# Three value loads of batch 0 tied behind the third block's reciprocal, and that block's finish moved ahead of unit 1's turns

## The chip, the cores and the metric

The kernel runs on one core of one Trainium2 chip. The metric is the device time of one execution in microseconds, the median over several runs. One execution was also taken with the hardware profiler; its views are what the argument below reads.

## The reference

Sparse causal attention over chunks, then a gated feed-forward layer. Inputs are q, k, v of 4 batches, 8 heads, 768 positions, 64 dimensions, in float32, and three weight matrices.

```python
k_chunks = k.reshape(B, H, nc, 32, D)                     # nc = 24
ub = sum over d of max(q*k_min[chunk], q*k_max[chunk])    # an upper bound for each chunk
top_chunks = argsort(where(causal, ub, -1e9))[..., -6:]   # six chunks of each query
scores = where(chosen & causal, (q @ k.T) / 8, -1e9)
attn = softmax(scores);  x = attn @ v                     # -> x: 3072 tokens x 512
out = (sigmoid(x @ w_gate) * (x @ w_val)) @ w_out         # 512 -> 1536 -> 512
```

## The kernel before, in words

**Tiling.** The 3072 tokens are cut into 8 units of 384 tokens, three blocks of 128 each. Unit 0 holds the first block of batches 0, 1 and 2 (the blocks that need no choice of chunks, since they see at most four). Unit 1 holds blocks 1 to 3 of batch 0. Unit 2 holds blocks 4 and 5 of batch 0 and the first block of batch 3; the rest follow.

**A first block** (function `first`) goes through these steps, with the names used below, `b` for the batch and `e` for one of two halves of the heads:

- `kf0_b`, `kf1_b`, `qf0_b`, `qf1_b`, `vf_b`: loads (issued by SP)
- `kfT_b`, `qfT_b`: turns on TensorE; `kf16_b`, `qf16_b`: casts; `scf_b`: scores; `expf_b_e`: exp (ScalarE, L751)
- `cmf_b_e`: the mask product, which sets what lies after the diagonal to zero (GpSimd, L753); `vc_b`: cast of the values (GpSimd)
- `pvf_b_e`: weights times values (TensorE, L760); `rzf_b_e`: reciprocal of the sums (VectorE, L766); `xf_b_e`: normalization (VectorE, L768)
- `xpsf_b_e`: turn (TensorE, L775); `xTf_b_e`: its eviction from PSUM into `xT_u0` (L452 on ScalarE, L454 on VectorE)

**Unit 1** is made ready at the same time: `k0_u1` to `k3_u1` and `q0_u1` to `q3_u1` are loads, `kn_`/`qn_` copies, `kT_`/`qT_` turns on TensorE, `kx0_`/`kx1_` minima and maxima (VectorE), `kt_`, `qf_`, `qm_`, `hk.._` and `hq.._` copies and casts. Its values are `v_0_1`, `v_0_2`, `v_0_3`: one load of 256 KB each (`load_v`, L667, SP), and one cast each (`v16_0_1` to `v16_0_3`, L673, GpSimd). The products `pv_u1_h` (L990) read them; of unit 1's heads, number 3 is the first in the order, after its mask product `cm_u1_3`.

**Weights** come by GpSimd's own DMA queue, with a cast from float32 to float16 on the way, in the order `wgp` (a quarter of the first third of w_gate), `wg0` (the rest of it), `wv0`, `wv1`, `wg1`, `wv2`, `wg2`, `wo0`, `wo1`, `wo2`. Everything else is loaded by SP's queue. Both queues use the same 16 DMA engines.

**The order** of all work is written out by hand: the string `ORDER` lists every operation with its engine (P TensorE, A ScalarE, V VectorE, G GpSimd, S SyncE, which issues loads and stores), and each engine runs its own in that order. `SLOTS` names each buffer. `TIES` adds waits: `a<b` makes the first instruction of `a` wait for the end of `b`:

```python
for b in ties.get(op.name, ()):
    tc.add_manual_dep(traced[n], ends[b], ..., reason="tie")
```

On SP the order around the change is: the loads of unit 1 (the last of them `k3_u1`, `q0_u1`, `k1_u1`), then `v_0_3`, `v_0_2`, `v_0_1`, `qf1_3`, `k0_u2`, `q2_u2`, `k1_u2`, and the other loads of unit 2. `fl_..` are products of constants that keep TensorE awake at the start.

Of the kernel before, what the change touches and what calls it, by code (L numbers as in the profile page):

```python
# [98 lines left out]
kf1_2=S kf0_1=S kfT_0=P kxf1=V fl_17=P fl_10=P fl_7=P kx0_u1_2=V kf16_0=V qf0_0=S qfT_0=P qf16_0=V qf1_1=S kf1_1=S kfT_1=P  # L99
kf16_1=V fl_15=P fl_16=P scf_0=P expf_0_1=A fl_19=P qf0_1=S qfT_1=P hq0=V ap1=V fl_14=P fl_9=P fl_13=P fl_11=P fl_18=P fl_12=P  # L100
qf16_1=V scf_1=P v10=G vf_0=S v16_0_0=G qf0_2=S qf1_2=S kf0_2=S expf_0_0=A cmf_0_0=G pvf_0_0=P rzf_0_0=V xf_0_0=V kx1_u1_2=V
cmf_0_1=G wgp=G kfT_2=P pvf_0_1=P qfT_2=P qf16_2=V rzf_0_1=V xf_0_1=V kxf0=V expf_1_0=A cmf_1_0=G vf_1=S vc_1=G pvf_1_0=P
rzf_1_0=V xpsf_0_0=P expf_1_1=A cmf_1_1=G pvf_1_1=P hkf0=G hk1_u1_2=A kf16_2=A scf_2=P expf_2_1=A expf_2_0=A k0_u1=S kn_u1_0=V
kT_u1_0=P xf_1_0=V fl_20=P fl_21=P wg0=G q3_u1=S qn_u1_3=A q2_u1=S rzf_1_1=V xf_1_1=V xpsf_1_1=P hq1=V xTf_1_1=V kx0_u1_0=V
kx1_u1_0=V vf_2=S wv0=G cmf_2_0=G fl_23=P xpsf_0_1=P fl_24=P fl_22=P fl_27=P xpsf_1_0=P vc_2=G xTf_1_0=V pvf_2_0=P rzf_2_0=V
xf_2_0=V q1_u1=S k3_u1=S kn_u1_3=G kT_u1_3=P hkp111=A q0_u1=S fl_28=P kx1_u1_3=V cmf_2_1=G pvf_2_1=P xpsf_2_0=P rzf_2_1=V xf_2_1=V
qT_u1_3=P qf_u1_3=V k1_u1=S qn_u1_1=A qT_u1_1=P xTf_0_0=A xTf_0_1=A qn_u1_2=A qn_u1_0=A kn_u1_1=G kT_u1_1=P kx1_u1_1=V kx0_u1_1=V
kt_u1_0=A qm_u1_3=A fl_25=P xpsf_2_1=P fl_26=P qT_u1_2=P v_0_3=S v_0_2=S v_0_1=S qf1_3=S k0_u2=S q2_u2=S k1_u2=S qf_u1_1=V
qf_u1_2=V v11=G wv1=G wg1=G hq0_u1_3=G qT_u1_0=P kt_u1_3=A hk0_u1_3=G hq1_u1_3=G wv2=G xTf_2_1=A xTf_2_0=A qf_u1_0=A qm_u1_0=A
g_u0_0=P g_u0_2=P kx0_u1_3=V kcr_f=V kcr_u1=V hkp101=V hq1_u1_0=V hkf1=V kt_u1_1=V hk0_u1_1=G wg2=G qm_u1_2=A qm_u1_1=A ub_u1=P  # L110
ubn0_u1=V ubm0_u1=V hq0_u1_1=A hq0_u1_2=A g_u0_3=P g_u0_1=P mx0_u1=V ap0_u1=V apt0_u1=V hqm0_u1_0=V v_u0_1=P v_u0_0=P v_u0_2=P
hq0_u1_0=A tanh_u0_2=A tanh_u0_1=A hg_u0_1=V ubn1_u1=V v_u0_3=P tanh_u0_3=A hg_u0_3=V ubm1_u1=V hg_u0_2=V tanh_u0_0=A hg_u0_0=V
# [257 lines left out]
sw0_u5_1<sw1_u5_0 sw1_u5_1<hg_u5_8 sw3_u5_2<c22_g4_u6 sw2_u5_2<c3_g2_u6 sw0_u45_1<c22_g2_u6 sw1_u45_1<c11_u5 sw0_u45_2<u4_u5  # L370
sw1_u45_2<c12_u5 sw3_u45_1<c22_u5 sw3_u45_2<c21_u5 tt0_u7<c11_u45 tt3_u7<c22_g1_u6 held_u6_2<hg_u6_8 sw2_u6_0<c11_g3_u7
sw2_u6_2<c4_g3_u7 sw1_u6_0<c12_g3_u7 sw2_u6_1<hg_u6_7 sw1_u67_0<sw0_u7_0 sw3_u7_0<hg_u7_4 sw1_u7_1<hg_u7_11 sw3_u7_2<sw1_u67_2
sw3_u67_2<c11_u7 sw3_u67_1<u4_u7 sw2_u67_2<c12_u7
"""


# [1080 lines left out]
```

## Time and profile before

| | |
|---|---|
| Median of 3 runs | 281.0 us (280.96 to 281.25) |
| Profiled execution, its own time | 279.88 us |
| Span of that execution, first to last instruction | 278.2 us |
| TensorE busy | 269.2 us (97%) |
| VectorE, ScalarE, GpSimd busy | 231.2, 180.4, 163.1 us |
| DMA moved | 34.70 MB, mean 125 GB/s |

In the rows below, times are microseconds from the start of the span. A row of the timeline gives start, duration, engine, line, operation, output and input, and how many instructions were merged (x3); in brackets stands the idle time before it and what ended it. PE is TensorE's matmul, PEld its weight load, DVE VectorE, ACT ScalarE, POOL GpSimd, SPq the issue of a DMA by SyncE. A DMA's time "to landing" counts from its issue to its last byte.

### The profile page before, as it was taken

The page shows a single profiled execution, that of the slowest core. Times are in us where ns is not written, and L with a number is a line of the kernel's source. Part 1 is how long each engine was busy: PE and PEld are TensorE (multiplying, and loading weights), DVE is VectorE, ACT ScalarE, POOL GpSimd, SP SyncE. Part 2 cuts the span into 40 slices and gives each one's busy share as a digit, 9 for nine tenths or more (in the row PEclk, how much of TensorE's full clock was granted, in tenths as well). Part 3 has the DMA queues.
Part 4 walks back from the last instruction along what each step waited for, and adds up shares of the span by engine and source line. Part 5 has one row for each costly group of instructions (what it writes and reads, how often), then busy time and mean ns, then how long its engine had stood idle before and what let it go on. Part 6 is the DMA issues. An engine that isn't in the chain of part 4 may idle for free.

```text
span 278.2 us, 7566 instructions
## 1 busy us (share of the span) xinstructions
PE 269.2 (97%) x2806; PEld 189.3 (68%) x2806; DVE 231.2 (83%) x686; ACT 180.4 (65%) x386; POOL 163.1 (59%) x262
## 2 busy tenths in 40 slices
PE   5979999999999999999999999999999999999995
PEld 3755658667755666557687657776888688778684
DVE  4799747687999998796999987978889998888985
ACT  6388969569858944468689979988983422341430
POOL 5797744639372873534669966724766467163440
PEclk9999999999999999999999999999999999999999
DMA  6999999999999598696896230100320033000304
GB/s 157 258 281 204 207 217 208 220 179 202 187 217 189 142 183 188 145 161 125 164 157 114 68 85 17 40 0 3 73 77 2 1 83 127 2 1 2 151 2 152
DMA packets 131717, 34.70 MB, mean 125 GB/s; under 512 B 119776, under 2 KB 128736, under 8 KB 131680
## 3 DMA queue, kind: packets, MB, share of 16 engines
q1 hardware_dynamic: 126912, 29.50, 50.6%
q0 software_dynamic: 4768, 4.72, 10.1%
q8 instruction: 22, 0.36, 0.5%
q14 instruction: 15, 0.12, 0.1%
HBM read 30.67 MB, written 6.29 MB: 133 GB/s over the span
## 4 chain that ended last, share of the span: by engine, by line
PE 87%; DMA 6%; DVE 5%; SPq 1%; issue 0%; POOL 0%; DVEq 0%
PE v_u L1259 20%; PE g_u L1259 15%; PE sc_u L957 12%; PE o_u L1308 11%; PE p_u L1082 10%; PE pv_u L990 7%; DMA wg<-in_moe_w_gate_dram 5%; PE p_g_u L1191 5%; PE ube_u L896 3%; DMA kf<-in_k_dram 1%; DVE xf L768 1%; PE kfT L709 1%; PE qfT L709 1%; PE fl L591 1%; DVE kx_u L681 1%; DVE kcr L681 1%
## 5 line engine op out<-in xcount | busy, mean ns | idle before, releaser
L968 ACT ACTIVATE att_u<-sc_u 128x512 f16<-128x512 f32 (+3 forms) x184 | 86.9, 573 | 8.6 <-PE sc_u L957 7.3
L1259 PE MATMUL v_u<-xT_u,wv 128*128 128x384 f16 x384 | 72.4, 326 | 0.0
L1280 DVE SCALAR_TENSOR_TENSOR hg_u<-gate_u,v_u 128x384 f16<-128x384 f16 x96 | 51.2, 545 | 19.3 <-ACT gate_u L1271 9.7
L1271 ACT ACTIVATE gate_u<-g_u 128x384 f16<-128x384 f32 x72 | 35.1, 499 | 40.3 <-PE g_u L1259 35.1
L1259 PE MATMUL g_u<-xT_u,wg 128*128 128x384 f16 x288 | 56.0, 326 | 0.9 <-ACT xT_u L452 0.5
L1259 PEld LDWEIGHTS <-wv 128*128 128x128 f16 x384 | 36.2, 98 | 20.3 <-issue 0.2
L974 POOL TENSOR_SCALAR_AFFINE_SELECT att_u<-att_u 128x384 f16<-128x384 f16 (+1 forms) x56 | 28.0, 509 | 37.4 <-ACT att_u L968 16.4
L1259 PEld LDWEIGHTS <-wg 128*128 128x128 f16 x288 | 26.7, 98 | 18.3 <-DMA wg<-in_moe_w_gate_dram 1.8
L1308 PE MATMUL o_u<-wo,hg_u 128*128 128x512 f16 x144 | 34.3, 379 | 0.0
L990 PE MATMUL pv_u<-v,att_u 128*128 128x65 f16 x640 | 26.3, 193 | 0.0
L990 PEld LDWEIGHTS <-att_u 128*128 128x128 f16 x640 | 24.2, 98 | 2.9 <-issue 0.6
L1228 DVE TENSOR_TENSOR f_g_u<-p_g_u,f_g_u 128x192 f32<-128x192 f32 (+1 forms) x72 | 24.9, 383 | 1.0 <-PE p_g_u L1191 0.4
L957 PE MATMUL sc_u<-hqe,hke 128*128 128x128 f16 (+2 forms) x220 | 25.1, 243 | 0.0
L957 PE MATMUL sc_u<-hqo,hko 128*128 128x128 f16 (+2 forms) x220 | 24.1, 243 | 0.0
L1308 PEld LDWEIGHTS <-hg_u 128*128 128x128 f16 x144 | 13.7, 98 | 13.4
L957 PEld LDWEIGHTS <-hke 128*128 128x128 f16 x220 | 16.5, 98 | 4.9 <-issue 0.6
L957 PEld LDWEIGHTS <-hko 128*128 128x128 f16 x220 | 16.4, 98 | 4.4
L673 POOL CAST v<-v 128x512 f16<-128x512 f32 x23 | 14.4, 627 | 5.8 <-DVE qf_u L863 1.8
L1271 ACT ACTIVATE gate_u<-f_g_u 128x384 f16<-128x384 f32 x24 | 11.9, 519 | 5.6 <-DVE hg_u L1280 2.9
L1011 DVE TENSOR_TENSOR x_u<-pv_u,rz_u 128x384 f16<-128x384 f32 (+1 forms) x28 | 14.6, 524 | 0.9 <-DMA xT_u<-x_u 0.6
L919 DVE MAX8 mx_u<-ubn_u 128x8 f32<-128x8 f32 (+16 forms) x152 | 12.7, 158 | 0.3
L1099 DVE SCALAR_TENSOR_TENSOR sw<-p_u,sw 128x256 f32<-128x256 f32 (+1 forms) x20 | 10.6, 528 | 2.4 <-PE p_u L1082 2.0
(187 smaller groups left out, 504.9 us busy)
## 6 DMA issues: line engine op xcount, KB each, us to landing
v<-in_v_dram SPq DMA_DIRECT2D x23, 256.0 KB, 4.7
k<-in_k_dram SPq DMA_DIRECT2D x12, 384.0 KB, 5.4
q<-in_q_dram SPq DMA_DIRECT2D x12, 384.0 KB, 5.9
out_dram<-osb_u SPq DMA_DIRECT2D x12, 256.0 KB, 3.3
out_dram<-sw SPq DMA_DIRECT2D x8, 256.0 KB, 2.1
wv<-in_moe_w_val_dram POOLq DMA_DIRECT2D x3, 512.0 KB, 9.8
wo<-in_moe_w_out_dram POOLq DMA_DIRECT2D x3, 512.0 KB, 17.6
qf<-in_q_dram SPq DMA_DIRECT2D x8, 128.0 KB, 3.3
```

The source lines that it names most:

```text
L673: plan.add(f"v16_{b}_{ib}", {POOL: pool(H * D)}, lambda e: nc.gpsimd.tensor_copy(v16[b % 2][:, ib, :, 0:D], at(t)), reads=[t], writes=[("v ...
L957: nc.tensor.matmul(at(t)[:, o:o + 128 * m], hk[b % 2][e_][:, p, 128 * jb:128 * jb + 128], hq[u.side][e_][:, p, 128 * x:128 * (x + m)], sta ...
L968: plan.add(f"exp_{u.name}_{h}_{y}", {ACT: act(n)}, lambda e, t=t, att=att, b0=b0, n=n: nc.scalar.activation(at(att)[:, b0:b0 + n], at(t), ...
L974: nc.gpsimd.affine_select(out=dv, in_=dv, compare_op=ALU.is_ge, fill=0.0, base=0, pattern=[[0, u.m], [1, 128]], channel_multiplier=-1)
L990: nc.tensor.matmul(at(pv)[:, last, x, :], at(att)[:, c:c + 128], v16[b % 2][:, jb, h, :], start=(jb == 0), stop=(jb == ib))
L1011: plan.add(f"x_{u.name}_{p}", {DVE: dve(u.t)}, lambda e: nc.vector.tensor_tensor(at(x_).rearrange("p a (e d) -> p e a d", e=2), at(pv)[:, ...
L1082: nc.tensor.matmul(at(to)[:, side], a(j)[:, i], b(j)[:, i], start=j == i == 0, stop=j == 2 and i == 1)
L1228: plan.add(f"{p}_{name}", {POOL: pool2(192 * n), DVE: dve(192 * n)} if slow else {DVE: dve(192 * n)}, lambda e: both(e).tensor_tensor(dst( ...
L1259: nc.tensor.matmul(at(t), w16[:, c, 128 * fb:128 * fb + 128], at(u.xt)[:, c, :], start=(c == 0), stop=(c == 3))
L1271: plan.add(f"tanh_{u.name}_{fb}", {ACT: act(T, not seven[0])}, lambda e, gv=gv, gate=gate: nc.scalar.activation(at(gate), gv(), AF.Tanh, s ...
L1280: plan.add(f"hg_{u.name}_{fb}", {DVE: dve(T)}, lambda e, vv=vv, gate=gate, hg=hg, fb=fb: nc.vector.scalar_tensor_tensor(at(hg)[:, fb % 2], ...
L1308: nc.tensor.matmul(at(o), at(hgs[fc // 2])[:, fc % 2, 128 * tb:128 * tb + 128], wo16[:, fc, lo:hi], start=(fc == 0), stop=(fc == NFB - 1))
```

## The change

One tie is added, `v_0_3<rzf_2_0`: the load `v_0_3`, and with it all that SP issues behind it, waits for the first reciprocal of the third block (batch 2). In `ORDER` the third block's operations move ahead of some of unit 1's, and `wgp` moves behind one mask product. By engine, before and after:

```
G  before: cmf_0_1 wgp cmf_1_0 vc_1 ... cmf_2_0 vc_2 kn_u1_3 cmf_2_1 kn_u1_1
   after:  cmf_0_1 cmf_1_0 wgp vc_1 ... cmf_2_0 vc_2 cmf_2_1 kn_u1_3 kn_u1_1
P  before: pvf_2_0 kT_u1_3 fl_28 pvf_2_1 xpsf_2_0 qT_u1_3 qT_u1_1 kT_u1_1 fl_25 xpsf_2_1 fl_26
   after:  pvf_2_0 fl_28 pvf_2_1 kT_u1_3 xpsf_2_0 qT_u1_3 xpsf_2_1 qT_u1_1 kT_u1_1 fl_25 fl_26
V  before: rzf_2_0 xf_2_0 kx1_u1_3 rzf_2_1 xf_2_1 qf_u1_3
   after:  rzf_2_0 xf_2_0 rzf_2_1 xf_2_1 kx1_u1_3 qf_u1_3
A  before: qn_u1_0 kt_u1_0 qm_u1_3 kt_u1_3 xTf_2_1 xTf_2_0 qf_u1_0
   after:  qn_u1_0 xTf_2_0 xTf_2_1 kt_u1_0 qm_u1_3 kt_u1_3 qf_u1_0
S  the same order
```

The diff, cut to the lines in which operations move:

```diff
-cmf_0_1=G wgp=G kfT_2=P pvf_0_1=P qfT_2=P qf16_2=V rzf_0_1=V xf_0_1=V kxf0=V expf_1_0=A cmf_1_0=G vf_1=S vc_1=G pvf_1_0=P
+cmf_0_1=G kfT_2=P pvf_0_1=P qfT_2=P qf16_2=V rzf_0_1=V xf_0_1=V kxf0=V expf_1_0=A cmf_1_0=G wgp=G vf_1=S vc_1=G pvf_1_0=P
...
-xf_2_0=V q1_u1=S k3_u1=S kn_u1_3=G kT_u1_3=P hkp111=A q0_u1=S fl_28=P kx1_u1_3=V cmf_2_1=G pvf_2_1=P xpsf_2_0=P rzf_2_1=V xf_2_1=V
-qT_u1_3=P qf_u1_3=V k1_u1=S qn_u1_1=A qT_u1_1=P xTf_0_0=A xTf_0_1=A qn_u1_2=A qn_u1_0=A kn_u1_1=G kT_u1_1=P kx1_u1_1=V kx0_u1_1=V
-kt_u1_0=A qm_u1_3=A fl_25=P xpsf_2_1=P fl_26=P qT_u1_2=P v_0_3=S v_0_2=S v_0_1=S qf1_3=S k0_u2=S q2_u2=S k1_u2=S qf_u1_1=V
-qf_u1_2=V v11=G wv1=G wg1=G hq0_u1_3=G qT_u1_0=P kt_u1_3=A hk0_u1_3=G hq1_u1_3=G wv2=G xTf_2_1=A xTf_2_0=A qf_u1_0=A qm_u1_0=A
+xf_2_0=V q1_u1=S k3_u1=S hkp111=A q0_u1=S fl_28=P cmf_2_1=G kn_u1_3=G pvf_2_1=P kT_u1_3=P xpsf_2_0=P rzf_2_1=V xf_2_1=V kx1_u1_3=V
+qT_u1_3=P xpsf_2_1=P qf_u1_3=V k1_u1=S qn_u1_1=A qT_u1_1=P xTf_0_0=A xTf_0_1=A qn_u1_2=A qn_u1_0=A xTf_2_0=A xTf_2_1=A kn_u1_1=G
+kT_u1_1=P kx1_u1_1=V kx0_u1_1=V kt_u1_0=A qm_u1_3=A fl_25=P fl_26=P qT_u1_2=P v_0_3=S v_0_2=S v_0_1=S qf1_3=S k0_u2=S q2_u2=S
+k1_u2=S qf_u1_1=V qf_u1_2=V v11=G wv1=G wg1=G hq0_u1_3=G qT_u1_0=P kt_u1_3=A hk0_u1_3=G hq1_u1_3=G wv2=G qf_u1_0=A qm_u1_0=A
...
-sw3_u67_2<c11_u7 sw3_u67_1<u4_u7 sw2_u67_2<c12_u7
+sw3_u67_2<c11_u7 sw3_u67_1<u4_u7 sw2_u67_2<c12_u7 v_0_3<rzf_2_0
```

## The prediction

> **What bounds the kernel now.** I read the page's busy times, then busy time by stretch, then the chain that ended last, then the timeline around the change, and last the landings of single loads.
>
> ```profile
> span 278.2 us, 7566 instructions
> PE 269.2 (97%) x2806; PEld 189.3 (68%) x2806; DVE 231.2 (83%) x686; ACT 180.4 (65%) x386; POOL 163.1 (59%) x262
> ...
> 0.00:36.00 36.00, 30.49 (x253) 20.36 (x254) 26.44 (x84) 25.64 (x52) 27.46 (x50) 1.00 1.08 221
> 36.00:120.00 84.00, 83.75 (x877) 54.35 (x875) 70.02 (x196) 56.40 (x128) 45.67 (x78) 1.00 1.01 189
> 120.00:200.00 80.00, 80.00 (x991) 55.51 (x990) 68.39 (x232) 70.49 (x144) 50.55 (x76) 1.00 0.43 82
> 200.00:278.20 78.20, 74.91 (x691) 59.09 (x689) 66.40 (x177) 27.87 (x65) 39.43 (x59) 1.00 0.16 55
> ```
>
> A stretch's row gives its length, then PE, PEld, DVE, ACT and POOL busy, the clock, the DMA share and GB/s. TensorE is the bound: of its 9.0 us idle, 5.5 lie before 36 us, 3.3 at the end, and 0.25 between 36 and 200. So a delay of TensorE near 36 us is hardly made up later. The DMA engines are full (share 1.01 and more) for the first 120 us: that is where a change in the order of loads can bite.
>
> ```profile
> 26.18 14.22 DMA wg<-in_moe_w_gate_dram
> 40.45 1.48 PE g_u L1259 x8
> ...
> 22.82 1.43 PE L1259 MATMUL g_u<-xT_u,wg 128*128 128x384 f16 x6 [0.51 <-ACT xT_u L452]
> 23.27 0.76 PEld L1259 LDWEIGHTS <-wg 128*128 128x128 f16 x6 [1.12 <-DMA wg<-in_moe_w_gate_dram]
> 22.00:26.00 4.00, 3.37 (x45) 1.42 (x44) 3.68 (x11) 3.96 (x11) 2.31 (x5) 1.00 1.22 206
> ```
>
> The chain passes through a load of w_gate that lands at 40.4, and unit 0's first gate products at 22.82 wait for the evictions of its x and for `wg0`. These are the waits that the change could shorten. Their whole worth is small: TensorE idles 0.63 us between 22 and 26, and 0.25 at 40.
>
> **The change part by part.** First, when the tie opens.
>
> ```profile
> 12.82 0.79 POOL L610 DMA_DIRECT2D wg<-in_moe_w_gate_dram  x1
> 12.86 1.08 ACT L751 ACTIVATE attf<-scf 128x512 f16<-128x512 f32 x2 [1.27 <-PE scf L746]
> 13.63 0.66 POOL L753 TENSOR_SCALAR_AFFINE_SELECT attf<-attf 128x512 f16<-128x512 f16 x1
> 15.91 0.80 POOL L612 DMA_DIRECT2D wg<-in_moe_w_gate_dram  x1
> 18.08 0.62 POOL L456 CAST vh<-vf 128x512 f16<-128x512 f32 x1
> 19.19 0.17 DVE L766 RECIPROCAL rzf<-pvf 128x4 f32<-128x4 f32 x1
> 19.79 0.56 DVE L681 TENSOR_REDUCE kx_u<-kT_u 128x12 f32<-128x384 f32 x1
> 22.13 0.65 ACT L452 COPY xT_u<-xpsf 128x256 f16<-128x256 f16 x2
> ```
>
> GpSimd issues `wgp` in the time in which it would wait for ScalarE's first exp of block 1, which ends near 13.40 (12.86 and half of 1.08). With `cmf_1_0` ahead, GpSimd starts it at 13.45 and `wgp` at 14.03, 1.2 us later; `vc_1` and all behind it, the issues of `wg0` and `wv0` too, come 0.6 us later (14.21 to 14.83), for GpSimd has no gap there up to the third block's value cast (18.08 to 18.70). Bound: 0 to 0.8, the issue's own 0.79. So `rzf_2_0`, which before ended at 19.36, ends at 20.0, and `v_0_3` goes out at 20.0 instead of 14.53. Behind it on SP stand the two other value loads, `qf1_3` and every load of unit 2.
>
> The moves on TensorE, VectorE and ScalarE bring the second half of block 2 forward past `kx1_u1_3` (0.56), a turn or two, and put two evictions (0.65 together) ahead of `kt_u1_0`, where ScalarE will also wait for their turns. I cost them at nothing: the next paragraphs show a wait of TensorE near 36 us that ends at a time set by a load, and whatever is won or lost before it only changes its length. If that cover is gone, they are worth between -0.6 (the idle time at 22 to 26) and +1.1 us (0.65 and some 0.4 of waiting).
>
> Now the loads.
>
> ```profile
> 14.53 4.84 SPq L667 DMA_DIRECT2D v<-in_v_dram  x3
> ...
> L667 SPq DMA_DIRECT2D v<-in_v_dram x1: 413/413/413, 14.5 to 14.5; - x1
> DMA to landing us min/median/max: 5.8/5.8/5.8
> ...
> L667 SPq DMA_DIRECT2D v<-in_v_dram x1: 3542/3542/3542, 15.8 to 15.8; - x1
> DMA to landing us min/median/max: 14.3/14.3/14.3
> ...
> L636 SPq DMA_DIRECT2D qf<-in_q_dram x1: 803/803/803, 19.5 to 19.5; - x1
> DMA to landing us min/median/max: 13.9/13.9/13.9
> ...
> L613 POOL DMA_DIRECT2D wv<-in_moe_w_val_dram x1: 780/780/780, 16.7 to 16.7; - x1
> DMA to landing us min/median/max: 9.8/9.8/9.8
> ...
> L613 POOL DMA_DIRECT2D wv<-in_moe_w_val_dram x1: 763/763/763, 20.4 to 20.4; - x1
> DMA to landing us min/median/max: 9.5/9.5/9.5
> ...
> 14.00:18.00 4.00, 2.39 (x32) 1.65 (x31) 3.65 (x12) 2.83 (x6) 4.00 (x7) 1.00 1.14 298
> ```
>
> `v_0_3` lands 5.8 us after its issue, before the bulk of the weights has begun to move: `wv0` lands at 26.5, `wv1` at 29.9. `v_0_1`, issued at 15.8 and let go by SP at 19.37, lands only at 30.1, and `qf1_3`, 128 KB behind it in the same queue, at 33.4. So once the weights run, SP's queue gets 128 KB through in 3.25 us, about 40 GB/s, where the engines moved 298 GB/s between 14 and 18. In the changed kernel `v_0_3` goes out at 20.0 and stands where `v_0_1` stood: it lands near 30.1. The two behind it need 6.5 us each: 36.6 and 43.1 for `v_0_1`. That is the late bound. The early bound: without the first two value loads in the way (512 KB, 1.7 us at 298 GB/s) `wg0` and `wv0`, themselves issued 0.6 later, are through up to 1.1 us sooner, while `wv1` can't be issued sooner; so the weights' queue may pause ahead of `wv1` for 0 to 1.1 us. In a pause the values pass at 298 GB/s; 1.1 us of it takes 328 KB, saves 8.2 us at 40 GB/s and costs 1.1, so `v_0_1` lands at 36.0. I take half of that pause, 0.5 us: 149 KB, 3.7 less 0.5, so 39.9.
>
> Who waits for it:
>
> ```profile
> 31.44 0.61 POOL L673 CAST v<-v 128x512 f16<-128x512 f32 x1
> 33.48 0.61 POOL L673 CAST v<-v 128x512 f16<-128x512 f32 x1 [0.74 <-DVE hqo L454]
> 34.20 0.99 POOL L974 TENSOR_SCALAR_AFFINE_SELECT att_u<-att_u 128x384 f16<-128x384 f16 x2
> 36.19 0.44 PE L990 MATMUL pv_u<-v,att_u 128*128 128x65 f16 x9
> ...
> 11.64 0.80 PE fl L591 x6
> ...
> L591 PE MATMUL fl<-ones x30: 269/396/421, 1.1 to 21.4; 128*128 128x256 f16 x30
> ```
>
> GpSimd casts `v_0_2` at 31.44 and `v_0_1` at 33.48; both will wait, and behind them on GpSimd stand `cm_u1_3` and `cm_u1_2` (34.20), without which `pv_u1_3` can't start, and TensorE runs in order. From the landing to `pv_u1_3`: the cast 0.61, a step of 0.11, one mask product 0.50, a step of 0.16, so 1.4 us. With 39.9 it starts at 41.3 instead of 36.19: **5.1 us**, between 1.2 (36.0) and 8.3 (43.1).
>
> A wait of 5 us may also cost TensorE its clock. The constant products took about 400 ns each at the start and 269 later, and the six at 11.64 took 133 ns apiece back to back: TensorE does start slow here. A restart after a long wait isn't in this trace. Bounds: 0, and half of the time from 1.1 to 11.64, 5.3. I take 1.5, near the low end, since after the wait TensorE is packed, while in its first ten microseconds it was fed in pieces. The Trainium skill (TensorE: Matmul & The Clock Gate, Part 1) says that about 3.4 us of idle time halve the clock and about 3.4 us of work restore it; by that this term would be an estimated 1.7 and the sum 0.2 higher.
>
> Off go TensorE's waits after 36 us that come from the weights: 0.25. The sum: 5.1 + 1.5 - 0.3 = +6.3 on the profiled execution's 279.88 (its span and 1.7 us around it), so 286.2. The median of the runs stands 1.1 above that execution: 281.0 + 6.3 = **287.3 us**.
>
> **The rivals.** *Faster: the values land in time.* If `v_0_1` lands by 34.8 (36.19 less 1.4), TensorE waits for nothing, and what is left is the shorter start: the idle 0.63 and 0.25 us at most, so 280.1. For it speaks that the first value load needed only 5.8 us, and that GpSimd asks for the last two 11.4 and 13.5 us after the new issue; against it, `v_0_1`'s 14.3 and `qf1_3`'s 13.9 us. It decides at a pause of 1.3 us or more in the weights' queue. The Trainium skill (DMA: Bandwidth & Descriptors, Anatomy of one DMA) fits a DMA at about 2.0 us and its bytes over 436 GB/s; by that fit, an estimate, the three would be in by 24 us and this rival would hold. The trace disagrees: 14.3 us for one such load beside the weights.
>
> *Slower still: unit 2's loads pile up too.*
>
> ```profile
> 40.97 0.40 POOL L456 COPY qn_u<-kq_u 128x256 f32<-128x256 f32 x1
> ...
> L647 SPq DMA_DIRECT2D kq_u<-in_q_dram x1: 1597/1597/1597, 23.1 to 23.1; - x1
> DMA to landing us min/median/max: 14.0/14.0/14.0
> ```
>
> `q2_u2` landed at 37.1, 7.0 us behind `v_0_1`; its copy on GpSimd began 7.5 us after the cast of `v_0_1`. Both move together, with 0.5 us to spare; if the queue spreads by half again (3.5 us) the turns of unit 2 wait 3 us more, and with the late bound the time is 281.0 + 8.3 + 1.5 + 3.0 - 0.3 = 293.5.
>
> *Nothing:* the tie opens before SP reaches the load. It would have to open by 14.53, and the third block's scores aren't even exponentiated then; 281.0.
>
> **How the numbers follow.** The forecast case, a wait of TensorE for `v_0_1`, holds 77 in 100: same queue, same neighbours, and the late landing is in the trace twice. Faster 13, pile-up 8, nothing 2. A measurement of this kernel can tell about 0.2%, 0.6 us, from no change. Faster 0.13; same 0.03, the last case and the edge of the first; slower 0.84. Range: the forecast's early bound (281.0 + 1.2 - 0.3 with no loss of clock, 281.9) to its late one with a clock loss of twice my value (281.0 + 8.3 + 3.0 - 0.3 = 292.0), drawn in to 282.0 and 291.5. It leaves out the faster case and most of the pile-up.
>
> **What would show it.** Right: the value loads issue near 20 us and land near 30, 35 and 40, where the first landed at 20 and the last at 30; GpSimd's third value cast waits for a DMA of v; TensorE idles some 5 us ahead of the `pv_u` products, is slow for a few microseconds behind it, and all later stretches are shifted and otherwise alike. `wg0` lands 1 to 2 us sooner, `wv1` not. Wrong: the third cast still near 34 us, or loads of v that land 7 us after their issue beside the weights; then the queue isn't shared as I read it.

## The result and the profile after

The changed kernel takes 283.7 us in the median of 21 executions (282.05 to 291.5), the kernel before beside it 281.0 (21 executions, 280.16 to 282.68). The ratio is 1.0075 [1.0057, 1.0092]; like every ratio below it leaves out executions that lie over 1.5% above the fastest of their kernel, here the seven above 287 (the medians stand 1% apart). So it is slower, as forecast, but by 2.7 us and not by 6.3.

The 21 times are two groups: 14 lie between 282.05 and 285.21, 7 between 287.55 and 291.5. The forecast of 287.3 falls into the gap. The profiled execution took 291.28 us and belongs to the upper group, so what it shows is the mechanism in its long form; profiles of the lower group follow with the repeats. First the page of the changed kernel:

```profile
span 289.5 us, 7563 instructions
PE 271.4 (94%) x2806; PEld 190.7 (66%) x2806; DVE 231.2 (80%) x686; ACT 180.4 (62%) x386; POOL 162.9 (56%) x262
```

Then its busy time by stretch, with the columns of before (length, PE, PEld, DVE, ACT, POOL, clock, DMA share, GB/s):

```profile
0.00:36.00 36.00, 30.34 (x253) 20.48 (x254) 26.54 (x84) 25.52 (x52) 23.96 (x43) 0.95 1.06 211
36.00:120.00 84.00, 74.90 (x759) 49.41 (x758) 60.81 (x163) 51.80 (x120) 43.91 (x78) 0.94 0.90 167
120.00:200.00 80.00, 80.00 (x974) 53.21 (x972) 68.35 (x238) 65.25 (x133) 49.09 (x72) 1.00 0.52 104
```

TensorE is busy for 30.34 us before 36 (before: 30.49) and without a gap from 120 to 200. In the second stretch it idles 9.1 us where it idled 0.25. The chain that ended last (start, duration, what) names the load:

```profile
16.16 4.64 DMA wg<-in_moe_w_gate_dram
20.80 23.54 DMA v<-in_v_dram
44.46 0.61 POOL v L673
45.07 0.48 POOL att_u L974
45.59 0.62 PE pv_u L990 x8
```

In the timeline stand the issue of the three value loads, their three casts, and what TensorE does behind them:

```profile
19.62 7.98 SPq L667 DMA_DIRECT2D v<-in_v_dram  x3
...
31.26 0.61 POOL L673 CAST v<-v 128x512 f16<-128x512 f32 x1 [1.37 <-DMA v<-in_v_dram]
...
37.95 0.61 POOL L673 CAST v<-v 128x512 f16<-128x512 f32 x1 [4.83 <-DMA v<-in_v_dram]
...
44.46 0.61 POOL L673 CAST v<-v 128x512 f16<-128x512 f32 x1 [5.21 <-DMA v<-in_v_dram]
...
45.59 0.62 PE L990 MATMUL pv_u<-v,att_u 128*128 128x65 f16 x8 [9.10 <-POOL att_u L974]
...
50.92 0.33 PE L1025 MATMUL xps_u<-ident,x_u 128*128 128x128 f16 x3
```

The loads go out from 19.6 and their casts follow one another by 6.7 and 6.5 us, each behind a wait for a DMA of v. TensorE's 9.10 us at `pv_u1_3` are the whole loss of its second stretch; the row names the mask product, which had itself waited for the cast, and the cast for the load. From `pv_u1_3` to the turns `xps_u1_3` it takes 5.33 us where before took 3.02, from 36.19 to this row of the kernel before:

```profile
39.21 0.33 PE L1025 MATMUL xps_u<-ident,x_u 128*128 128x128 f16 x3
```

The stretches of the changed kernel show the clock (the number before the DMA share), 0.80 in the wait and 0.50 behind it:

```profile
38.00:42.00 4.00, 0.00 (x0) 0.00 (x0) 0.00 (x0) 0.00 (x0) 1.25 (x2) 0.80 1.22 200
...
46.00:50.00 4.00, 4.00 (x25) 2.25 (x23) 1.82 (x5) 0.98 (x2) 1.15 (x4) 0.50 1.01 230
```

So this execution lost 9.4 us up to `pv_u1_3` and 2.3 us to the clock, 11.7 together, and ended 11.4 later than the profiled execution of before.

### The profile page after: what moved, and what is told of

Same layout as the page of the kernel before. It is cut to its first block, busy times and chain, and to the rows that moved or that the text cites. A ratio compares the mean times of both kernels' runs of the same rounds, so it can differ in the third digit from the quotient of the medians.

```text
span 289.5 us, 7563 instructions
## 1 busy us (share of the span) xinstructions
PE 271.4 (94%) x2806; PEld 190.7 (66%) x2806; DVE 231.2 (80%) x686; ACT 180.4 (62%) x386; POOL 162.9 (56%) x262
## 4 chain that ended last, share of the span: by engine, by line
PE 84%; DMA 11%; POOL 1%; DVE 1%; issue 1%; SPq 0%; ACT 0%; DVEq 0%; POOLq 0%
PE v_u L1259 20%; PE g_u L1259 15%; PE sc_u L957 12%; PE o_u L1308 11%; PE p_u L1082 9%; DMA v<-in_v_dram 8%; PE pv_u L990 7%; PE p_g_u L1191 5%; PE ube_u L896 2%; DMA wg<-in_moe_w_gate_dram 2%; DMA kf<-in_k_dram 1%; PE kfT L709 1%; PE qfT L709 0%; DVE ox L1099 0%; PE xps_u L1025 0%
## 5 line engine op out<-in xcount | busy, mean ns | idle before, releaser
L1280 DVE SCALAR_TENSOR_TENSOR hg_u<-gate_u,v_u 128x384 f16<-128x384 f16 x96 | 51.1, 544 | 29.3 <-ACT gate_u L1271 20.0
L1259 PE MATMUL v_u<-xT_u,wv 128*128 128x384 f16 x384 | 73.3, 329 | 0.0
L1259 PE MATMUL g_u<-xT_u,wg 128*128 128x384 f16 x288 | 56.7, 329 | 0.1
L1259 PEld LDWEIGHTS <-wv 128*128 128x128 f16 x384 | 36.6, 99 | 21.0 <-issue 1.2
L974 POOL TENSOR_SCALAR_AFFINE_SELECT att_u<-att_u 128x384 f16<-128x384 f16 (+1 forms) x56 | 28.0, 509 | 37.7 <-ACT att_u L968 17.5
L990 PE MATMUL pv_u<-v,att_u 128*128 128x65 f16 x640 | 26.9, 195 | 9.1 <-POOL att_u L974 9.1
L673 POOL CAST v<-v 128x512 f16<-128x512 f32 x23 | 14.4, 627 | 17.2 <-DMA v<-in_v_dram 11.4
L863 DVE STREAM_TRANSPOSE qf_u<-q 128x384 f32<-128x384 f32 (+2 forms) x28 | 11.7, 436 | 1.3 <-DMA q<-in_q_dram 1.2
```

What stands on the lines that cost most here:

```text
L974: nc.gpsimd.affine_select(out=dv, in_=dv, compare_op=ALU.is_ge, fill=0.0, base=0, pattern=[[0, u.m], [1, 128]], channel_multiplier=-1)
L990: nc.tensor.matmul(at(pv)[:, last, x, :], at(att)[:, c:c + 128], v16[b % 2][:, jb, h, :], start=(jb == 0), stop=(jb == ib))
L1259: nc.tensor.matmul(at(t), w16[:, c, 128 * fb:128 * fb + 128], at(u.xt)[:, c, :], start=(c == 0), stop=(c == 3))
L1280: plan.add(f"hg_{u.name}_{fb}", {DVE: dve(T)}, lambda e, vv=vv, gate=gate, hg=hg, fb=fb: nc.vector.scalar_tensor_tensor(at(hg)[:, fb % 2], ...
```

## The experiments

**The changed kernel again, three times.** They show the lower group, and how the sizes scatter.

> The changed kernel as it is, to see an execution that is not among its longest. Theory A (the value loads share the DMA engines with the weights, and the last of them lands at a time that differs from run to run): times spread between 282 and 291.5 us as before; in the profile the length of the wait ahead of the first pv_u product and the landing of the third value load move together: an execution of 283 us has the load landing near 36 to 38 and a wait of 1 to 3 us, with the granted clock hardly lowered. Theory B (the new order makes the start slower and the loads matter only now and then): the wait ahead of pv_u is nearly nothing in an execution of 283 us, and TensorE is behind already at 30 us by 2 us.

> The changed kernel once more, beside the kernel with constants ahead of pv_u and on the same chip. Theory A (a race between the value loads and wv1 on each DMA engine): short executions of 282 to 284.5 and about a third of 287 to 292, whichever chip.

> The changed kernel on the same chip, for comparison: 282 to 284.5, and long executions of 287 to 292 in up to a third.

Measured: 283.66 (281.8 to 292.15, 12 executions, 3 of them above 287), ratio 1.0058 [1.0027, 1.0088]; 283.15 (282.46 to 284.43, 6, none above 287), 1.0080 [1.0055, 1.0104]; 283.89 (282.02 to 291.73, 6, 2 above 287), 1.0096 [1.0062, 1.0131]. Their profiled executions took 283.51, 283.68 and 282.02. Timeline of the first, the same steps:

```profile
18.91 5.59 SPq L667 DMA_DIRECT2D v<-in_v_dram  x3
...
37.57 0.61 POOL L673 CAST v<-v 128x512 f16<-128x512 f32 x1 [4.81 <-DMA v<-in_v_dram]
...
38.70 0.42 PE L990 MATMUL pv_u<-v,att_u 128*128 128x65 f16 x8 [2.79 <-POOL att_u L974]
...
43.27 0.33 PE L1025 MATMUL xps_u<-ident,x_u 128*128 128x128 f16 x3
```

Of the second:

```profile
39.11 0.42 PE L990 MATMUL pv_u<-v,att_u 128*128 128x65 f16 x8 [2.58 <-POOL att_u L974]
...
42.11 0.34 PE L1025 MATMUL xps_u<-ident,x_u 128*128 128x128 f16 x3
```

And of the third:

```profile
20.03 4.71 SPq L667 DMA_DIRECT2D v<-in_v_dram  x3
...
37.91 0.42 PE L990 MATMUL pv_u<-v,att_u 128*128 128x65 f16 x8 [1.06 <-POOL att_u L974]
```

Where the last value load lands near 37 instead of 44, TensorE waits 1.06 to 2.79 us and not 9.10. Behind a wait of 2.79 the clock fell for a while (4.57 us to `xps_u1_3`, 1.55 more than before), behind 2.58 it did not (3.00); the last section shows that the length of the wait alone does not decide this. The granted clock of the stretch from 38 to 42 says the same, in the first and in the second repeat:

```profile
38.00:42.00 4.00, 3.30 (x26) 2.01 (x27) 1.11 (x3) 0.79 (x2) 2.26 (x6) 0.64 1.21 213
```

```profile
38.00:42.00 4.00, 2.89 (x32) 1.89 (x32) 1.17 (x4) 0.98 (x2) 2.68 (x6) 1.00 1.21 211
```

**The tie without the moves, and the moves without the tie.** The first is the kernel before with the tie, the second the changed kernel without it:

```diff
 before, one tie more:    +v_0_3<rzf_2_0
 after, that tie removed: -v_0_3<rzf_2_0
```

> The kernel before with the tie alone, the order as before. Theory A: the same delay of the value loads, opened some 0.3 us sooner (the reciprocal at 19.4): slower by 1 to 10 us, median 283 to 285, with a spread like the changed kernel's. Theory B: within 0.5 us of the kernel before.

> The changed kernel without the tie: the third block's operations stay ahead. Theory A: within 0.6 us of the kernel before, and a spread as small as its (280.2 to 282.7), since the value loads go out at 14.5 again. Theory B: 282.5 to 284, the changed kernel's time.

Measured: the tie alone 289.07 (283.33 to 290.94, 12), ratio 1.0116 [1.0074, 1.0159]; 7 of its 12 executions lie above 287. The moves alone 281.43 (280.42 to 282.85, 12), 0.9990 [0.9963, 1.0017]. The timeline of the tie alone, in its profiled execution of 290.94:

```profile
45.79 0.62 PE L990 MATMUL pv_u<-v,att_u 128*128 128x65 f16 x8 [9.32 <-POOL att_u L974]
```

So the whole loss comes from the tie, and the moves cost and bring nothing by themselves, although without the tie no wait hides them. With the tie, the moves made the upper group rarer (7 of 12 without them, 3 of 12 with them on the same chip); with such counts that is a hint and no more. The timeline of the moves alone:

```profile
37.14 0.43 PE L990 MATMUL pv_u<-v,att_u 128*128 128x65 f16 x9
...
40.16 0.33 PE L1025 MATMUL xps_u<-ident,x_u 128*128 128x128 f16 x3
```

This execution took 280.76, near the 281.0 of before, and `pv_u1_3` starts at 37.14, 0.95 later than in the profiled execution of before, with no wait for a value load. That matters below.

**How many of the three loads are held.** The kernel before, with the tie at the second or at the third load alone:

```diff
+v_0_2<rzf_2_0        (two loads held)
+v_0_1<rzf_2_0        (one load held)
```

> The kernel before with the tie on v_0_2: the first value load goes out at 14.9, two are held until 19.4. Theory A: 6.5 us less on the slowest DMA engine than with three held: the last lands at 37 to 38 at the latest, a wait ahead of pv_u of 0 to 2.5 us; 281 to 283.5, and nothing above 286. If the number of held loads doesn't matter: the times of the tie alone, 283 to 291.

> The kernel before with the same tie on the third value load alone (v_0_1). In the kernel before SP let that load go only at 19.37, so the tie holds it no longer than the queue did. Theory A, which counts the loads that are held past the start of the weights: no change, within 0.5 us, the load lands near 30 as before. Theory B: no change either. A third view, that any wait of SP on the reciprocal costs: slower by 1 us or more.

> The tie on the third value load alone, again, since it came out 0.3% below the kernel before with an interval that ends just under 1. Theory A: nothing is held longer than by the queue, 0 to 0.3% faster at best; I expect the interval to hold 1.

Measured: two held 283.02 (280.18 to 285.0, 12), 1.0059 [1.0027, 1.0091]; one held 280.77 (280.26 to 281.49, 10), 0.9971 [0.9946, 0.9995], and on the repeat 280.84 (280.24 to 283.93, 12), 1.0003 [0.9985, 1.0021]. Beside the 289.07 for three held loads the time goes with the number of loads behind the tie: what costs is how many 256 KB loads must pass beside the weights. The gain of the one held load was not there on the repeat. Its landing was not as expected: it came at 35.5 in the first profiled execution and at 38.1 in the repeat's, not near 30. So one held load uses up the slack ahead of `pv_u1_3`, and sometimes more; the repeat's profiled execution took 283.93, and its timeline shows the late cast:

```profile
38.24 0.61 POOL L673 CAST v<-v 128x512 f16<-128x512 f32 x1 [4.67 <-DMA v<-in_v_dram]
```

**A pause made by holding the weights.** If the weights beside them are what slows the value loads, holding the weights must let them through. The issues of `wv1`, `wg1` and `wv2` are moved behind VectorE's `kcr_u1`, in the changed kernel and in the kernel before:

```diff
-... v11=G wv1=G wg1=G hq0_u1_3=G ... hq1_u1_3=G wv2=G ... kcr_u1=V ...
+... v11=G hq0_u1_3=G ... hq1_u1_3=G ... kcr_u1=V wv1=G wg1=G wv2=G ...
+wv1<kcr_u1
```

> The changed kernel with wv1, wg1 and wv2 issued some 3 us later (tied behind the range product kcr_u1, near 24 us), so that the weights' queue stands still for some 3 us on every DMA engine while the value loads are in theirs. Theory A (in the long executions one DMA engine, which is late with its share of wv0, has no pause, and the values on it take turns with the weights): the three value loads land by 30, the third cast starts before 35, no wait ahead of the first pv_u product, and no execution above 286. The weights are 3 us later and TensorE waits for wv1 near 31 and for wg1 near 35 instead, 2 to 3.5 us in all: 282.5 to 285. If the sharing of the engines were not the cause (the loads slow by themselves): the casts as late as in the changed kernel, and executions of 288 to 291 remain.

> The kernel before with wv1, wg1 and wv2 held until kcr_u1, no tie on the value loads. The price of the held weights alone: TensorE waits for wg1 and the later weights; as much as the changed kernel with the same hold, 281.5 to 283.

Measured: the changed kernel with the pause 282.41 (280.96 to 286.98, 12), 1.0050 [1.0018, 1.0082]; the kernel before with it 282.31 (281.56 to 284.25, 8), 1.0064 [1.0036, 1.0092]. The value loads by line in the first (duration of the issue, first and last start; then from issue to landing):

```profile
L667 SPq DMA_DIRECT2D v<-in_v_dram x3: 368/530/3137, 19.6 to 20.7; - x3
...
DMA to landing us min/median/max: 5.2/5.7/6.3
```

The same view of the changed kernel itself:

```profile
L667 SPq DMA_DIRECT2D v<-in_v_dram x3: 368/614/6806, 19.6 to 20.8; - x3
...
DMA to landing us min/median/max: 11.5/17.7/23.5
```

Issued at the same times, the three loads land in 5.2 to 6.3 us instead of 11.5 to 23.5 when the weights stand aside. The wait for v is gone, and another has come in its place, in the waits of TensorE between 28 and 45 us (us in total, times, longest):

```profile
PE g_u L1259 <- DMA wg<-in_moe_w_gate_dram: 2.2, 2, 1.8
```

With the weights held, the tie costs nothing more: the versions with and without it cost the same within their intervals (1.4 and 1.8 us by the ratios), the price of the late weights. That the weights moving at the same time are what slows the value loads is shown by this. That the two meet in the DMA engines, and not in the memory behind them, is read from the counts of pieces in the last section; no run parts the two. One of the 12 executions with the pause took 286.98, where none above 286 was expected; it was not profiled.

**When the tie opens.** In the changed kernel, the tie is set on an earlier and on a later step, and the earlier one also with the pause:

```diff
 earlier:            -v_0_3<rzf_2_0  +v_0_3<rzf_1_1
 later:              -v_0_3<rzf_2_0  +v_0_3<xf_2_1
 earlier and pause:  -v_0_3<rzf_2_0  +v_0_3<rzf_1_1  +wv1<kcr_u1, issues moved as above
```

> The changed kernel with the tie on the second block's last reciprocal (rzf_1_1, near 17.3 us) in place of the third block's first (19.9). Theory A: the value loads come to the DMA engines near 19.5, together with wg0 and wv0, and the last lands some 2.5 us sooner than in the changed kernel, 33 to 41; a median of 281 to 283 and fewer executions above 286. If any opening behind unit 1's loads costs the same: 283.7 again, with the same share of long executions.

> The changed kernel with the tie on xf_2_1, the third block's last normalization, near 21, some 1 us later. Theory A: the loads reach the DMA engines near 23.3 and fewer packets pass before and in the pause: the last lands 1 us later in short executions (38.5), 283.5 to 285.5, long ones as many or more.

> The kernel with the early tie (rzf_1_1) and with wv1, wg1 and wv2 held until kcr_u1 near 24 us. If the lost pause made the early tie slow: the loads land by 28, no wait ahead of pv_u, 281 to 283.5. If not: 285 to 289 as with the early tie alone.

Measured: earlier 287.69 (284.98 to 288.87, 6), 1.0221 [1.0167, 1.0274]; later 284.38 (283.2 to 286.19, 4), 1.0140 [1.0090, 1.0190]; earlier with the pause 283.07 (280.87 to 283.67, 10), 1.0063 [1.0035, 1.0092]. The first missed what was expected of it: loads issued 3.3 us sooner (from 16.3) made the kernel 4 us slower. The view by line shows it:

```profile
L667 SPq DMA_DIRECT2D v<-in_v_dram x3: 368/544/4791, 16.3 to 17.4; - x3
...
DMA to landing us min/median/max: 9.4/15.6/21.6
```

The last load goes out at 17.4 and lands at 38.9. The reason stands in the landings of each load's sixteen shares, one for each DMA engine. The table is read from the trace's records of landings: for each profiled execution the earliest and latest of the sixteen, in us.

```
                        wv0            first load     second load    third load     wv1
changed, 291.28         23.3 - 26.3    24.4 - 31.1    25.4 - 37.8    37.7 - 44.3    27.9 - 29.9
tie alone, 290.94       23.3 - 26.2    24.2 - 31.3    25.1 - 37.9    37.8 - 44.5    27.7 - 29.6
again, 283.51           22.7 - 25.2    23.6 - 25.8    24.5 - 30.9    34.8 - 37.4    27.1 - 29.5
again_2, 283.68         23.5 - 26.0    24.4 - 26.7    25.3 - 31.2    35.6 - 37.8    27.8 - 30.4
later, 283.2            23.4 - 25.3    24.3 - 26.1    25.3 - 30.7    35.3 - 37.3    27.8 - 30.0
earlier, 284.98         24.8 - 25.9    21.3 - 25.7    22.8 - 32.3    32.3 - 38.9    27.8 - 29.2
again_3, 282.02         23.8 - 24.8    24.7 - 25.7    25.6 - 26.6    35.0 - 36.6    28.4 - 29.3
with the pause, 283.0   23.3 - 23.9    24.2 - 24.8    25.1 - 25.8    26.1 - 27.0    30.4 - 31.6
```

Between the end of its share of `wv0` and the start of `wv1` an engine serves the value loads alone, and each passes in about 0.9 us; once `wv1` runs, each takes some 6.6. A load has landed when its slowest engine is through, so it is a matter of counting how many of the three loads that engine passes before `wv1`: none in the two long executions (steps of 6.7, then 6.5), one in `again`, `again_2`, and with the later and the earlier tie, two in `again_3`, three with the pause. In the long execution of the changed kernel 13 of the 16 engines were through with the second load by 25.9; 15 of the 16 shares of `wv0` had landed by 25.4 and the last at 26.3. That it is the same engine that then gave the landing of the value loads is inferred, since the landings don't name the engines. SP lets the third load go later there too: its issue ends at 27.60, against 24.50 and 24.74 in the first and third repeat.

The count alone does not give the landing in `again_3`. Two loads are in at 26.6 there, and 6.6 more would be 33.2; the third load landed at 36.6, because it did not move in between. By the trace's packet records the 2048 pieces of the first two loads are through at 26.25 and the first piece of the third starts at 28.05, 3.3 us after SP let it go. In the other executions of the changed kernel the earliest share of the third load lands at 34.8 or later as well. So the third load, which sets the time, was never in the pause; only with the weights held does it follow the second without a gap. Why its pieces start so late is not known.

With the earlier tie the second load meets `wv0`, whose first share lands later than elsewhere (24.8), so that next to no pause is left ahead of `wv1`; held weights give it back, and the time falls from 287.69 to 283.07 (on different chips, each beside the kernel before). The loads are in by 29.3 then, where 28 was expected. That the weights behind `wv0` decide here too is shown by this pair. The profiled execution of the earlier tie is the quickest of its six; the five of 286.94 to 288.87 were not profiled. That a few late engines make the upper group is what the records of two long and six shorter executions agree with; no run took the late engines away, and why they are late isn't known.

**TensorE kept busy through the wait.** 24 constant products (`flx`) just ahead of `pv_u1_3`, in the changed kernel (twice) and in the kernel before:

```diff
-cm_u1_3=G pv_u1_3=P
+cm_u1_3=G flx=P pv_u1_3=P        (flx: 24 products of ones16 into a free PSUM slot)
```

> The changed kernel with 24 products of constants (2.6 us of TensorE work) ahead of the first pv_u product, to part the wait from the clock. Theory A with a clock term: in short executions (a wait of 2 to 3 us) TensorE never stands still, the clock stays up, and 1 to 1.7 us come back: the shorter executions near 281.5 to 282.5. In long executions 6 us of the wait are left and the clock falls all the same: 288 to 291.5 remain. If the clock costs nothing: no change in the short executions, or up to 0.5 us slower where the load lands early.

> The kernel with 24 constant products ahead of the first pv_u product, on the same chip as the changed kernel. On another chip it had no execution above 284.1 in 12. If that was the chip or chance: about the same share of long executions as the changed kernel beside it, those 1 us shorter at most. If the constants themselves shorten long ones (by keeping the clock through the first 2.6 us of the wait): long executions of 286 to 289 at most.

> Control: the same 24 products put into the kernel before, where TensorE doesn't wait at that place. TensorE is the bound there, so their 2.6 us should come out in full: 283.2 to 283.9. If it came out under 1 us, TensorE has more slack behind 36 us than its busy time says, and a wait could be made up.

Measured: changed kernel 283.14 (282.17 to 284.08, 12), 1.0081 [1.0055, 1.0107], and 283.91 (282.37 to 286.81, 6), 1.0088 [1.0058, 1.0117]; kernel before 282.64 (282.11 to 283.24, 4), 1.0059 [1.0036, 1.0081]. Timeline of the changed kernel with them:

```profile
35.53 2.78 PE L600 MATMUL flx<-ones 128*128 128x256 f16 x24
38.37 0.43 PE L997 MATMUL pv_u<-v,att_u 128*128 128x65 f16 x9
...
41.39 0.34 PE L1032 MATMUL xps_u<-ident,x_u 128*128 128x128 f16 x3
```

The clock is kept (3.02 us to `xps_u1_3`, as before), but no time is won against the changed kernel: in two of the three profiled executions of the lower group there was no clock to win, and the products themselves end at 38.31, about 1 us after `pv_u1_3` could have gone (the cast of `v_0_1` starts at 36.11 here, and in the executions without the products `pv_u1_3` starts 1.1 us behind that cast). In the kernel before the same 2.8 us of work on the bound engine cost only 1.7, less than was expected. Timeline of that one:

```profile
36.01 2.78 PE L600 MATMUL flx<-ones 128*128 128x256 f16 x24
38.85 0.43 PE L997 MATMUL pv_u<-v,att_u 128*128 128x65 f16 x9
...
41.87 0.34 PE L1032 MATMUL xps_u<-ident,x_u 128*128 128x128 f16 x3
```

`pv_u1_3` is 2.66 us later than in the profiled execution of before, and this execution took 282.11, 2.23 more than that one. Part of the difference may lie in what is compared: next section. That no execution of the changed kernel with the products lay above 287 (none of 18, against 12 of 45 without them) is not explained; in their two profiled executions the value load was not late (landed at 36.0 and 36.5).

## Why the prediction was right in its direction and wrong in its size

The step that failed is the landing of `v_0_1`, put at 39.9 by a pause of half a microsecond ahead of `wv1`; two smaller terms of the sum failed beside it. Right were the other steps of the mechanism, each seen in the trace.

- *The tie opens at 20.0*: the loads go out from 19.6 (18.9 to 20.0 in the repeats).
- *6.5 us for each value load beside the weights*: 6.7 and 6.5 between the casts of the profiled execution; the late bound of 43.1 for `v_0_1` is 1.2 and 1.4 us short of where the two long executions have it (44.3 and 44.5), since the first load landed at 31.1 and 31.3 and not at 30.1.
- *1.4 us from landing to `pv_u1_3`*: 44.3 to 45.59 and 37.4 to 38.70, 1.3 both times.
- *The moves at nothing*: 0.9990 [0.9963, 1.0017] with their cover gone, inside the bounds of -0.6 to +1.1.
- *TensorE's waits for weights behind 36 us go*: in the profiled execution, of 84 us from 36 on, 9.10 are idle, and all 9.10 stand at `pv_u1_3`. By this row the pile-up of unit 2's loads did not come either, for its turns don't wait.
- *A delay of TensorE near 36 us is hardly made up later*: the time from `xps_u1_3` to the end lies between 238.5 and 240.0 us in all eighteen profiled executions, whatever came before. Nine of them (us, from the timelines and spans):

```
                      pv_u1_3   xps_u1_3   from there to the end of the span   execution
before                 36.19     39.21       239.0                              279.88
moves alone            37.14     40.16       238.9                              280.76
again_3                37.91     40.91       239.4                              282.02
again_2                39.11     42.11       239.9                              283.68
again                  38.70     43.27       238.5                              283.51
two loads held         38.96     44.56       238.7                              285.00
earlier                40.20     44.73       238.6                              284.98
tie alone              45.79     50.59       238.5                              290.94
changed                45.59     50.92       238.6                              291.28
```

The rival in which the values land in time needed `v_0_1` by 34.8; the earliest landing seen in the changed kernel is 36.6, and 36.0 with the constants. Where it was forced, by the held weights, the wait for the late weights took its place. The fit that the prediction set beside this rival (the Trainium skill, DMA: Bandwidth & Descriptors, Anatomy of one DMA) is stated for DMAs that GpSimd issues, and these loads are SP's.

Wrong were three terms of the sum.

1. **The pause ahead of `wv1`**, taken as 0.5 us of 0 to 1.1, as if the queue had one pause, the saving grew with its length, and all of it came off the landing of `v_0_1`. The pause was there: `wv0` landed at 24.8 to 26.3 where before had 26.5, and `wv1` no more than 0.6 sooner. But the runs showed a count: the slowest engine passes none, one or two loads in the pause, and `v_0_1` lands at 44.3 to 44.5, 37.3 to 37.8 or 36.6. `v_0_1` itself never used the pause: in `again_3` its pieces began to move at 28.05, 3.3 us after SP let it go, and in the four profiled executions of the changed kernel its first share landed at 34.8 to 37.7. No profiled execution of the changed kernel lands near the 39.9 of the sum; those that took 287.55 to 288.97 us, which may, were not profiled. That the median belongs to the early end and not to the late one is a matter of which group is the larger, 14 executions to 7; nothing in the prediction could tell that. So the three repeats start `pv_u1_3` 1.7 to 2.9 us later than before, and the long executions 9.4 and 9.6, against 5.1.
2. **The clock**, taken as +1.5. It was 1.55 in one repeat, 0 in two, and 2.3 in the long execution (1.8 in that of the tie alone). The waits of the lower group were shorter than forecast, which follows from the first term; one of 2.58 us kept the clock and one of 2.79 lost it. The rule of the Trainium skill (TensorE: Matmul & The Clock Gate, Part 1) gave 1.7 for one idle period; in the first repeat the trace agrees within 0.2, but a wait of 2.79 us was enough for it, and the page speaks of 3.4.
3. **The 1.1 us between the profiled execution and the median**, added on top. The profiled execution of before was quicker than all 21 executions of the comparison (279.88 against 280.16 to 282.68). With the 239 us from `xps_u1_3` on and 1.7 around the span, the median of 281.0 has its `xps_u1_3` near 40.3 and its `pv_u1_3` near 37.3, as in the execution with the moves alone. That is an estimate and not seen: no execution of before at its median was profiled, and with the 238.5 to 240.0 of all profiled executions `pv_u1_3` could stand anywhere from 36.3 to 37.8. But such a late start is swallowed by the wait for `v_0_1`, which ends at a time set by a load; the prediction said so of the moves and did not apply it to the scatter. The constant products in the kernel before, whose 2.8 us cost 1.7, fit this. So this term is argued, and the first two are measured.

Put together with the measured values: `pv_u1_3` at 37.9 to 39.1, 3.0 us to `xps_u1_3` or 4.6 with the clock lost, 238.5 to 239.9 to the end and 1.7 around the span give the 282.0 to 283.7 of the three repeats; the median of 283.7 lies at their upper end, as it must with a third of the executions in the upper group.

## What to carry to other kernels

When a load is held back, ask what its queue will meet on the DMA engines at the new time: three loads of 256 KB that took 6 us alone took 12 to 24 beside the weights, and the last one set the start of the bound engine. Where a time hangs on a race that is won or lost load by load, don't put the forecast halfway between the bounds; work out both ends and ask which is the likelier. And sum against an execution like the median one, since a wait that ends at a fixed time swallows the scatter ahead of it.

## What the runs showed of the hardware that was not expected

- **Two queues share a DMA engine piece by piece.** Read from the packet records, from 26 to 29 us the kernel before moves 62 to 74 pieces of 256 bytes of the value loads in half a microsecond beside 74 to 79 pieces of 1024 bytes of the weights; the queue with the small pieces gets under 40 GB/s of 200. In the changed kernel, from 23.5 to 25 us, it is 428 to 477 pieces of values to 13 to 21 of the weights.
- **SP stalls in the issue of a load.** The three issues took 7.98 us in the profiled execution of the changed kernel, 5.59 and 4.71 in two repeats; the last of these issues is the long one (6.81, 4.28 and 3.62). It ended late where an engine was late, which suggests that SP waits for the slowest engine; no run shows that by itself.
- **The granted clock changes in steps of 3.41 us.** In the trace's record of the clock the stretch at half speed behind `pv_u1_3`'s wait is 3.41 us long in the first repeat, 6.83 with two loads held (a wait of 2.91), 10.24 in the profiled execution of the changed kernel (9.10). Waits of 2.14, 2.16 and 2.58 us left it whole. But the length alone does not decide. Continued backward in steps of 3.41 us from its changes, the record cuts these waits: the 2.91 us lay 2.0 ahead of an edge and 0.9 behind it, the 2.58 us 1.7 and 0.9. By the timelines TensorE was busy for 0.63 us (first repeat) and 1.37 us (two loads held) of the step that ended in the fall, and for 1.67, 1.75 and 1.78 us of the steps after which the clock stayed. That holds around this wait; between 12 and 18 us the clock fell after steps with 1.80 to 1.92 us busy. The Trainium skill (TensorE: Matmul & The Clock Gate, Part 1) describes a free-running window of 3413 ns, and the lengths agree.
- **A load of 256 KB is far from its size over the bandwidth.** The fit of the Trainium skill (DMA: Bandwidth & Descriptors, Anatomy of one DMA), about 2.0 us and the bytes over 436 GB/s, is stated for DMAs that GpSimd issues; carried over to this load of SP's it would give an estimated 2.6 us. The runs show 5.2 to 6.3 with the weights held and 11.5 to 23.5 beside them.
